# The words between the steps of a weight conversion, held in PSUM

## The chip, the core and the metric

The kernel runs on one core of a Trainium2 chip. Its engines are TensorE (PE: matmuls, PEld: weight loads), VectorE (DVE), ScalarE (ACT), GpSimd (POOL) and SyncE (SP, which issues all of the DMAs here). SBUF is the working memory; PSUM, eight banks of 128 partitions by 512 words of four bytes, takes what the matmuls write. The metric is the device time of one execution in microseconds.

## The reference

All of it is computed from float32 or float64 arrays of standard normal numbers, scaled. The weights arrive as 64-bit floats, seen by the kernel as pairs of 32-bit words.

```python
def sm_attn(qq, kk, vv):            # softmax attention, scale 1/sqrt(64)
    s = scale * np.matmul(qq, kk.transpose(0, 1, 3, 2))
    a = np.exp(s - np.max(s, axis=-1, keepdims=True))
    return np.matmul(a / (np.sum(a, axis=-1, keepdims=True) + 1e-09), vv)
p_packed = sm_attn(p, k, v)                  # 8 batches, 8 heads, 32 packed rows, 576 tokens
x = sm_attn(q, p_packed, p_packed)           # -> (4608, 512)
xn = x / np.sqrt(np.mean(x * x, axis=-1, keepdims=True) + 1e-06) * rms_g
g = xn @ w_gate                              # 512 -> 1536
x = (g * sigmoid(g) * (xn @ w_val)) @ w_out  # first MLP, 1536 -> 512
h = x @ w_in                                 # 512 -> 2048
out = (h * sigmoid(1.702 * h)) @ w_out2      # second MLP, 2048 -> 512
```

## The kernel before, in words

**Stages.** A start stage computes the attention of the first batches and begins the first MLP's weights. The first MLP (`mlp1`) then runs over four units `u` of two batches each, and within a unit over twelve slices `j` of 128 of the 1536 hidden columns. While it works on one unit, steps of the next unit's attention are put between its pieces; `run` yields the estimated nanoseconds of TensorE that a piece takes, and the main loop at the end spends them on attention steps. The second MLP (`mlp2`) comes last, over nine tiles of 512 tokens and sixteen slices of the 2048 hidden columns. The order of instructions on each engine is set by a scheduler at build time that starts from the order in the program and its own estimates of time; at run time every engine goes through its queue in order.

**Precision.** Most products are made of three matmuls on pairs "high, low" (`Wh, Wl` and so on): the high part is a rounded copy made by ScalarE, the low part is the difference, made by VectorE or GpSimd.

**PSUM.** Until the second MLP, pool `mm` has five banks under one tag, `mm`, handed out anew as they come free; pool `ap` has the other three for the attention. In the first MLP `mm` serves `ps_w` (L622, the slice's gate and value weights times the packed rows, read by ACT at L624 and DVE at L625), `ps_g` (L653, gate and value, read by ACT at L660 and DVE at L661 and L663) and `ps_o` (L684, the projection back to 512, read by ACT at L698 or L691, or DVE at L694). In the start stage, attention tiles take part of the `mm` banks too.

**Conversions.** `convert` makes a "high, low" pair out of raw 64-bit words: ScalarE takes the absolute value of the top words as a float (L105) into a tile `w`; VectorE works on it in four steps (L106 to L109: a lower bound, two shifts, the sign bits, the three bits from the low words); ScalarE makes the rounded copy (L110), and GpSimd the difference (L111). There are 104 conversions. In the first MLP `piece` converts its weights, 256 columns at a time, 72 in all, in the start stage and the first unit; the pairs go to DRAM and are read back for the later units. From the last unit on, `early` (in `mlp2`) converts the first nine slices of the second MLP's weights, 512 columns at a time, 18 in all, and `main` the other 14 when the second MLP runs and PSUM is laid out anew.

**POOL beside it.** GpSimd also makes `Hl` (L669) and adds into `acc` (L700) in the first MLP, in some 1.4 us each.

Of the kernel before, what the change touches and what calls it, by code (L numbers as in the profile page):

```python
# [9 lines left out]
F32 = mybir.dt.float32  # L10
F32R = mybir.dt.float32r
I32 = mybir.dt.int32
AF = mybir.ActivationFunctionType
ALU = mybir.AluOpType
# [5 lines left out]
LEAST_WORD = 2.0**-15  # L20


def fl(t):

    return t.bitcast(F32)
# [3 lines left out]
def tile_pack_attention__then__two_mlps(  # L29
# [14 lines left out]
    nc = tc.nc  # L44
    B, H, S, D = q.shape
    NP = p.shape[2]
    DM = H * D
# [6 lines left out]
    P = 128  # L54
# [40 lines left out]
    g_sb = const.tile([P, NPAIR], F32, name="g_sb")  # L95
    mhalf = const.tile([P, NC], F32, name="mhalf")

    def convert(pool, r, parts, n):


        top, low = r[:, :, 1], r[:, :, 0]
        w = pool.tile([P, n], I32, tag="w", name="w", bufs=3 if n < DM else 2)
        wf = w.bitcast(F32)
        shaped = wf if len(parts[0].shape) == 2 else wf.rearrange("p (i f) -> p i f", f=P)
        nc.scalar.activation(wf, top.bitcast(F32), AF.Abs)  # L105
        nc.vector.tensor_scalar(wf, wf, LEAST_WORD, None, op0=ALU.max)  # L106
        nc.vector.tensor_scalar(w, w, 5, 2, op0=ALU.logical_shift_left, op1=ALU.logical_shift_right)  # L107
        nc.vector.scalar_tensor_tensor(w, top, -(1 << 30), w, op0=ALU.bitwise_and, op1=ALU.bitwise_or)  # L108
        nc.vector.scalar_tensor_tensor(w, low, 29, w, op0=ALU.logical_shift_right, op1=ALU.bitwise_or)  # L109
        nc.scalar.copy(parts[0], shaped)  # L110
        nc.gpsimd.tensor_sub(parts[1], shaped, fl(parts[0]))  # L111

# [410 lines left out]
    def mlp1(cv, lp, mm, getL, getAT):  # L523
# [3 lines left out]
        HD = DM // 2  # L527
# [18 lines left out]
        raw = {}  # L546
# [20 lines left out]
        def piece():  # L567

            n = done[1]
            if n >= len(pieces):  # L570
                return False
            kind, j, c, h, _ = pieces[n]
            if j >= used[kind] + (WGB if kind == "wg" else G):
                return False
            done[1] += 1
            if (c, h) == (0, 0):
                tiles[kind, j] = new(kind, j)
            t = tiles[kind, j]
            if kind == "wg":
                parts = [t[:, x, 2 * h : 2 * h + 2, c * P : (c + 1) * P] for x in range(2)]  # L580
            else:
                parts = [t[:, x, h * HD : (h + 1) * HD] for x in range(2)]
            convert(cv, raw.pop(n), parts, HD)
            fetch()
            if n + 1 == len(pieces) or pieces[n + 1][:2] != (kind, j):
                nc.sync.dma_start((wg_d if kind == "wg" else wo_d)[j], fl(t))
                (wg if kind == "wg" else wo)[j] = tiles.pop((kind, j))
            return True

        def have(d, s):  # L590
            while s not in d:
                assert piece()
# [166 lines left out]
        return fetch, piece, run  # L759


    def mlp2(pre):
        xt = {}

        def load_x(t, pool):
# [18 lines left out]

        wi, wo = {}, {}
        raw = {}

        def load_w(n):
            f, x = divmod(n, 2)
# [17 lines left out]
                wi[f] = [w[:, y].rearrange("p (i f) -> p i f", f=P) for y in range(2)]  # L807

        def split_w(n, w):
            convert(pre, raw.pop(n), (w[:, 0], w[:, 1]), DM)  # L810
            load_w(n + 2)

        def keep(n, pool):
# [69 lines left out]
                    nc.sync.dma_start(out[t * TT + r * P : t * TT + (r + 1) * P, :], ob)  # L883

        def main(wp, xp):
            seq = [(t, f) for t in range(NTT) for f in range(NF2)]
            for n, (t, f) in enumerate(seq):
                if f == 2:
                    load_x(t + 1, pre if t % 2 else xp)
                if NF2 - 6 <= f < NF2 - 2:  # L890
                    split_x(t + 1, f + 6 - NF2)
                if t == 0:
                    if f == 0:
                        todo = list(range(4 + 2 * NEARLY, 2 * NF2))
                    for e in range(2, 5) if f == 0 else (f + 4,):
                        for x in range(2):
                            if e < 2 + NEARLY:
                                nc.sync.dma_start(fl(keep(2 * e + x, wp)), w2_d[e][:, x])
                up(t, f)
                if t == 0 and todo:  # L900
                    split_w(todo[0], keep(todo[0], wp))
                    todo.pop(0)
                if n >= 2:
                    down(*seq[n - 2])
            down(*seq[-2])
            down(*seq[-1])
# [5 lines left out]
    with ExitStack():  # L912
# [8 lines left out]
        with ExitStack() as st1:  # L921
            cv = st1.enter_context(tc.tile_pool(name="cv", bufs=1, side="left"))
            lp = st1.enter_context(tc.tile_pool(name="lp", bufs=1, side="left"))
            mm = st1.enter_context(tc.tile_pool(name="mm", bufs=MMB, space=PSUM, side="left"))
            st2 = ExitStack()
            ap = st2.enter_context(tc.tile_pool(name="ap", bufs=8 - MMB, space=PSUM, side="right"))
            at = st2.enter_context(tc.tile_pool(name="at", bufs=1, side="right"))
            Ls, ATs = {}, {}

            def begin(u):  # L930
                Ls[u] = tuple(lp.tile([P, NPAIR, P], F32R, tag=f"L{x}", name=f"L{x}", bufs=2) for x in "hl")
                ATs[u] = [
                    [lp.tile([P, S], F32, tag=f"AT{o}{g}", name=f"AT{o}{g}", bufs=1) for g in range(NG)]
                    for o in range(2)
                ]

            turn = [0]
            starting = [True]

            def psum():  # L940
                turn[0] += 1
                if starting[0] and turn[0] % 8 < MMB:
                    return mm.tile([P, 512], F32, tag="mm", name="ps_at")
                return ap.tile([P, 512], F32, tag="at", name="ps_at")

            def act(calls):
                for f, *args in calls:
                    f(*args)

            def unit(u):  # L950
                begin(u)
                n = 2 * NG * u
                seq = range(n, n + 2 * NG)
                return stages(seq, n + 2 * NG if u + 1 < NU else None, seq[NG - 1 :: NG])

            with tc.tile_pool(name="at2", bufs=1, side="left") as at2:
                start, stages = attention(at, [at2], lp, psum, Ls.get, ATs.get)
                fetch, piece, run = mlp1(cv, lp, mm, Ls.get, ATs.get)
                begin(0)
                todo = start(PERIOD, 2 * NG)  # L960
                while todo[0][0] < 0:
                    act(todo.pop(0)[1])
                nc.sync.dma_start(g_sb, rms_g.rearrange("(i p) -> p i", p=P))
                spent = CONV
                for _ in range(FETCH):
                    act(todo.pop(0)[1])
                for _ in range(3):
                    fetch()
                while todo[0][0] < LEADING:
                    time, calls = todo.pop(0)  # L970
                    act(calls)
                    while time > spent:
                        piece()
                        spent += PACE
                todo = [calls for _, calls in todo]
            starting[0] = False
            pools["main"] = st1.enter_context(tc.tile_pool(name="main", bufs=1, side="left"))
            u, ahead = 0, None
            every = EVERY / len(todo)
            spent, done = 0.0, 0.0  # L980
            for what in run():
                if what == "attention":
                    for calls in todo:
                        act(calls)
                    todo = []
                elif what == "next":
                    todo = unit(1)
                    every = 130000.0 / len(todo)
                elif what == "unit":
                    u += 1  # L990
                    if u + 1 < NU:
                        todo = unit(u + 1)
                        every = 143000.0 / len(todo)
                    elif u + 1 == NU:
                        st2.close()
                        pre = ctx.enter_context(tc.tile_pool(name="pre", bufs=1, side="right"))
                        early, second = mlp2(pre)
                        ahead = early()
                    spent = 0.0
                else:  # L1000
                    if ahead is not None and u == NU - 1:
                        next(ahead, None)
                    spent += what
                    done += what
                    while todo and spent >= every:
                        spent -= every
                        act(todo.pop(0))
                    while done >= PIECE:
                        done -= PIECE
                        piece()  # L1010
# [48 lines left out]
```

## Time and profile before

| | us |
|---|---|
| Time, median of three runs (1798.51 to 1803.16) | 1799.77 |
| The profiled execution's own time | 1803.39 |
| Its span, from the first to the last instruction | 1801.6 |
| PE busy | 1714.9 (95%) |
| DVE busy | 969.9 (54%) |
| ACT busy | 697.0 (39%) |
| POOL busy | 511.7 (28%) |

Durations come from one profiled execution on the chip. In the sliced view each digit is a slice's busy share in tenths (9 is 90% or more), and PEclk the granted clock of TensorE in tenths of full speed. In a group, the columns behind the shapes are the count, the engine's busy time in us, the mean ns of one instruction, and the engine's idle time just before them with what ended it. The ends of matmuls are modelled, so that neighbouring ones overlap in their records; neighbouring DVE instructions overlap by some 0.1 us too.

### The profile page before, as it was taken

The numbers are of one execution on the slowest core, as the hardware profiler recorded it, in microseconds if no ns is written. First come the engines' busy times: TensorE is split into PE (matmuls) and PEld (weight loads), VectorE is DVE, ScalarE is ACT, GpSimd is POOL, SyncE is SP. The second block draws the span as 40 slices with busy tenths as digits, with TensorE's granted clock in tenths as the row PEclk, the third lists the DMA queues.
The fourth block names the chain that finished last, engine by engine and source line by source line (L and its number), as shares of the span: only waits on it lengthen the run. The fifth ranks groups of instructions, "written<-read, shape, count | busy, mean of one in ns | idle before, by whom it ended". The sixth has DMA issues, their size and how long they took to land.

```text
span 1801.6 us, 26222 instructions
## 1 busy us (share of the span) xinstructions
PE 1714.9 (95%) x9976; PEld 1520.3 (84%) x9976; DVE 969.9 (54%) x1971; ACT 697.0 (39%) x1644; POOL 511.7 (28%) x470
## 2 busy tenths in 40 slices
PE   7798888999999999988899999999999999999998
PEld 5587877999999999978799788888888888888887
DVE  6979999856656666688955482122222222222221
ACT  5665655665555655556544331111111111111111
POOL 2546665644554345444544230000000000000000
PEclk9989998999999999999999999999999999999999
DMA  9654445454434542268731731010101010000000
GB/s 239 187 175 148 130 142 201 148 162 134 132 115 135 161 124 94 71 205 280 261 130 43 263 94 47 1 47 1 47 1 47 1 47 17 31 1 24 1 24 24
DMA packets 154462, 186.26 MB, mean 103 GB/s; under 512 B 87648, under 2 KB 124512, under 8 KB 147296
## 3 DMA queue, kind: packets, MB, share of 16 engines
q1 hardware_dynamic: 154336, 184.58, 32.0%
q8 instruction: 79, 1.29, 0.3%
q14 instruction: 47, 0.39, 0.1%
HBM read 139.46 MB, written 45.09 MB: 102 GB/s over the span
## 4 chain that ended last, share of the span: by engine, by line
PE 78%; DVE 16%; issue 2%; DMA 2%; ACT 2%; SPq 1%; POOL 0%; ACTq 0%; DVEq 0%; POOLq 0%
PE ps_dn L873 22%; PE ps_up L854 22%; PE ps_o L684 13%; PE ps_g L653 12%; DVE w L108 3%; PE ps_w L622 3%; DVE w L109 2%; PE ps_at L264 2%; DVE Wl L625 2%; DVE w L107 2%; DVE w L106 2%; PE ps_at L253 2%; DVE th L663 1%; PE ps_at L309 1%; DVE th L661 1%
## 5 line engine op out<-in xcount | busy, mean ns | idle before, releaser
L854 PE MATMUL ps_up<-xh,wi 128*128 128x512 f32 x1152 | 381.7, 393 | 2.3 <-DMA wi<-w 1.6
L873 PE MATMUL ps_dn<-wo,gh 128*128 128x512 f32 x1152 | 356.6, 391 | 0.0
L684 PE MATMUL ps_o<-Hh,wo 128*128 128x288 f32 x1536 | 332.1, 302 | 19.3 <-DVE th L661 9.0
L860 DVE CAST gh<-gf 128x512 fp32r<-128x512 f32 x144 | 62.4, 433 | 508.1 <-ACT gf L857 508.0
L857 ACT ACTIVATE gf<-ps_up 128x512 f32<-128x512 f32 x144 | 85.9, 597 | 610.3 <-PE ps_up L854 589.6
L684 PEld LDWEIGHTS ps_o<-Hh,wo 128*128 128x128 f32 x1536 | 255.5, 191 | 24.8 <-DVE th L661 9.9
L653 PE MATMUL ps_g<-Aqh,Wh 128*128 128x288 f32 x768 | 238.9, 312 | 23.5 <-ACT Wh L624 10.0
L854 PEld LDWEIGHTS ps_up<-xh,wi 128*128 128x128 f32 x1152 | 216.2, 188 | 52.0 <-POOL wo L111 2.0
L873 PEld LDWEIGHTS ps_dn<-wo,gh 128*128 128x128 f32 x1152 | 216.3, 188 | 47.5
L653 PE MATMUL ps_g<-Aql,Wh 128*128 128x288 f32 x768 | 229.5, 299 | 0.0
L684 PE MATMUL ps_o<-Hl,wo 128*128 128x288 f32 x768 | 228.2, 299 | 0.0
L653 PE MATMUL ps_g<-Aqh,Wl 128*128 128x288 f32 x768 | 228.1, 299 | 0.0
L854 PE MATMUL ps_up<-xl,wi 128*128 128x512 f32 x576 | 225.8, 392 | 0.0
L873 PE MATMUL ps_dn<-wo,gl 128*128 128x512 f32 x576 | 224.6, 391 | 0.0
L669 POOL TENSOR_TENSOR Hl<-th,Hh 128x576 fp32r<-128x576 f32 x96 | 141.0, 1469 | 235.4 <-ACT Hh L668 228.5
L653 PEld LDWEIGHTS ps_g<-Aqh,Wh 128*128 128x128 f32 x768 | 147.8, 193 | 32.0 <-ACT Wh L624 10.6
L700 POOL TENSOR_TENSOR acc<-acc,add 128x576 f32<-128x576 f32 x90 | 133.5, 1486 | 64.9 <-ACT add L698 64.8
L625 DVE TENSOR_TENSOR Wl<-ps_w,Wh 64x512 fp32r<-64x512 f32 x192 | 131.8, 687 | 30.9 <-ACT Wh L624 27.2
L653 PEld LDWEIGHTS ps_g<-Aql,Wh 128*128 128x128 f32 x768 | 147.8, 192 | 0.0
L653 PEld LDWEIGHTS ps_g<-Aqh,Wl 128*128 128x128 f32 x768 | 146.5, 192 | 0.5 <-DVE Wl L625 0.2
L684 PEld LDWEIGHTS ps_o<-Hl,wo 128*128 128x128 f32 x768 | 146.7, 191 | 0.1
L624 ACT CAST Wh<-ps_w 64x512 fp32r<-64x512 f32 x192 | 111.2, 580 | 59.5 <-PE ps_w L622 39.8
(146 smaller groups left out, 2649.2 us busy)
## 6 DMA issues: line engine op xcount, KB each, us to landing
wg<-wg SPq DMA_DIRECT2D x48, 1024.0 KB, 5.1
wo<-wo SPq DMA_DIRECT2D x48, 512.0 KB, 4.1
x<-acc SPq DMA_DIRECT2D x32, 288.0 KB, 2.4
out_dram<-ob SPq DMA_DIRECT2D x36, 256.0 KB, 2.0
vn<-in_v_dram SPq DMA_DIRECT2D x16, 512.0 KB, 5.3
qn<-in_q_dram SPq DMA_DIRECT2D x64, 128.0 KB, 4.0
raw<-in_moe_w_in_dram SPq DMA_DIRECT2D x16, 512.0 KB, 4.1
raw<-in_moe_w_out_dram SPq DMA_DIRECT2D x16, 512.0 KB, 3.8
```

Of the source, the lines that this page charges most:

```text
L108: nc.vector.scalar_tensor_tensor(w, top, -(1 << 30), w, op0=ALU.bitwise_and, op1=ALU.bitwise_or)
L622: nc.tensor.matmul(ps[:, a], st[:, i], mv[:, i], start=n == 0, stop=n == 2)
L624: nc.scalar.copy(Wh[rows, :, g], src)
L625: nc.vector.tensor_sub(Wl[rows, :, g], src, fl(Wh[rows, :, g]))
L653: nc.tensor.matmul(ps, st[:, o, g, c * P : (c + 1) * P], mv[:, g, cols], start=n == 0, stop=n == 3 * NG - 1)
L669: nc.gpsimd.tensor_sub(Hl, th, fl(Hh))
L684: nc.tensor.matmul(ps, st[:, m * P : (m + 1) * P], mv[:, cols], start=n == 0, stop=n == 3 * len(ss) - 1)
L700: nc.gpsimd.tensor_add(acc[o, m], acc[o, m], t)
L854: nc.tensor.matmul(ps, st[:, i], mv[:, i], start=n == 0, stop=n == 3 * NM - 1)
L857: nc.scalar.activation(gf, ps, AF.Gelu_apprx_sigmoid)
L860: nc.vector.tensor_copy(gh, gf)
L873: nc.tensor.matmul(pacc[r], st[:, r * P : (r + 1) * P], mv, start=f == 0 and n == 0, stop=f == NF2 - 1 and n == 2,)
```

## The change

`convert` gets a pool of banks. Where one is given, it takes a tile of 128 x 512 words of tag `mm` and uses its first `n` columns as `m`: L106 reads `w` in SBUF and writes `m` in PSUM, L107 and L108 read and write `m`, and L109 reads `m` and writes `w` in SBUF, from where L110 and L111 go on as before. The low and top words (`raw`) stay in SBUF. The number of instructions is the same. `piece` always gives `mm`; the second MLP's conversions give it while `early` runs and no longer once `main` does. In these the tile `m` is one more user of the five banks.

```diff
--- before.py
+++ after.py
@@ -95,18 +95,20 @@
     g_sb = const.tile([P, NPAIR], F32, name="g_sb")
     mhalf = const.tile([P, NC], F32, name="mhalf")
 
-    def convert(pool, r, parts, n):
+    def convert(pool, r, parts, n, banks=None):
+
 
 
         top, low = r[:, :, 1], r[:, :, 0]
         w = pool.tile([P, n], I32, tag="w", name="w", bufs=3 if n < DM else 2)
         wf = w.bitcast(F32)
         shaped = wf if len(parts[0].shape) == 2 else wf.rearrange("p (i f) -> p i f", f=P)
+        m = w if banks is None else banks.tile([P, 512], I32, tag="mm", name="between")[:, :n]
         nc.scalar.activation(wf, top.bitcast(F32), AF.Abs)
-        nc.vector.tensor_scalar(wf, wf, LEAST_WORD, None, op0=ALU.max)
-        nc.vector.tensor_scalar(w, w, 5, 2, op0=ALU.logical_shift_left, op1=ALU.logical_shift_right)
-        nc.vector.scalar_tensor_tensor(w, top, -(1 << 30), w, op0=ALU.bitwise_and, op1=ALU.bitwise_or)
-        nc.vector.scalar_tensor_tensor(w, low, 29, w, op0=ALU.logical_shift_right, op1=ALU.bitwise_or)
+        nc.vector.tensor_scalar(m.bitcast(F32), wf, LEAST_WORD, None, op0=ALU.max)
+        nc.vector.tensor_scalar(m, m, 5, 2, op0=ALU.logical_shift_left, op1=ALU.logical_shift_right)
+        nc.vector.scalar_tensor_tensor(m, top, -(1 << 30), m, op0=ALU.bitwise_and, op1=ALU.bitwise_or)
+        nc.vector.scalar_tensor_tensor(w, low, 29, m, op0=ALU.logical_shift_right, op1=ALU.bitwise_or)
         nc.scalar.copy(parts[0], shaped)
         nc.gpsimd.tensor_sub(parts[1], shaped, fl(parts[0]))
 
@@ -580,7 +582,7 @@
                 parts = [t[:, x, 2 * h : 2 * h + 2, c * P : (c + 1) * P] for x in range(2)]
             else:
                 parts = [t[:, x, h * HD : (h + 1) * HD] for x in range(2)]
-            convert(cv, raw.pop(n), parts, HD)
+            convert(cv, raw.pop(n), parts, HD, mm)
             fetch()
             if n + 1 == len(pieces) or pieces[n + 1][:2] != (kind, j):
                 nc.sync.dma_start((wg_d if kind == "wg" else wo_d)[j], fl(t))
@@ -759,7 +761,7 @@
         return fetch, piece, run
 
 
-    def mlp2(pre):
+    def mlp2(pre, banks):
         xt = {}
 
         def load_x(t, pool):
@@ -784,6 +786,7 @@
 
         wi, wo = {}, {}
         raw = {}
+        leading = [True]
 
         def load_w(n):
             f, x = divmod(n, 2)
@@ -807,7 +810,7 @@
                 wi[f] = [w[:, y].rearrange("p (i f) -> p i f", f=P) for y in range(2)]
 
         def split_w(n, w):
-            convert(pre, raw.pop(n), (w[:, 0], w[:, 1]), DM)
+            convert(pre, raw.pop(n), (w[:, 0], w[:, 1]), DM, banks if leading[0] else None)
             load_w(n + 2)
 
         def keep(n, pool):
@@ -883,6 +886,7 @@
                     nc.sync.dma_start(out[t * TT + r * P : t * TT + (r + 1) * P, :], ob)
 
         def main(wp, xp):
+            leading[0] = False
             seq = [(t, f) for t in range(NTT) for f in range(NF2)]
             for n, (t, f) in enumerate(seq):
                 if f == 2:
@@ -994,7 +998,7 @@
                     elif u + 1 == NU:
                         st2.close()
                         pre = ctx.enter_context(tc.tile_pool(name="pre", bufs=1, side="right"))
-                        early, second = mlp2(pre)
+                        early, second = mlp2(pre, mm)
                         ahead = early()
                     spent = 0.0
                 else:
```

## Rows read from the trace of the kernel before

**Rows 1.** The page's view in 40 equal slices.

```profile
PE   7798888999999999988899999999999999999998
...
DVE  6979999856656666688955482122222222222221
...
PEclk9989998999999999999999999999999999999999
```

**Rows 2.** Windows: busy us of PE, PEld, DVE, ACT, POOL; clock, DMA share, GB/s.

```profile
0.00:60.00 60.00, 48.26 (x232) 35.10 (x232) 40.21 (x120) 35.71 (x114) 20.30 (x40) 1.00 0.94 236
60.00:340.00 280.00, 235.49 (x1564) 218.13 (x1565) 258.24 (x548) 167.83 (x452) 165.62 (x166) 0.93 0.51 161
400.00:780.00 380.00, 380.00 (x2871) 370.87 (x2871) 244.00 (x552) 216.93 (x536) 177.20 (x159) 1.00 0.40 126
780.00:900.00 120.00, 98.36 (x672) 92.31 (x671) 110.79 (x179) 65.84 (x139) 57.64 (x38) 0.96 0.74 252
```

**Rows 3.** The chain of waits from 180 to 260 us: its shares by line.

```profile
by line: DVE w L108 13.7%; DVE w L109 10.3%; DVE Wl L625 9.0%; DVE w L107 8.6%; PE ps_g L653 7.9%; issue 7.1%; DVE th L661 5.0%; DVE th L663 4.5%; DVE w L106 4.3%; PE ps_w L622 3.7%; PE ps_at L264 3.5%; DVE kTl L134 2.6%; PE ps_at L412 2.3%
```

**Rows 4.** DVE's groups by shape, from 60 to 340 us.

```profile
L108 DVE SCALAR_TENSOR_TENSOR w<-raw,w 128x256 int32<-128x256 int32 x61 | 47.0, 774 | 0.3
L109 DVE SCALAR_TENSOR_TENSOR w<-raw,w 128x256 int32<-128x256 int32 x61 | 44.6, 734 | 0.4
L625 DVE TENSOR_TENSOR Wl<-ps_w,Wh 64x512 fp32r<-64x512 f32 x48 | 32.8, 686 | 1.5 <-ACT Wh L624 0.7
L107 DVE TENSOR_SCALAR w<-w 128x256 int32<-128x256 int32 x61 | 31.1, 511 | 0.4
L106 DVE TENSOR_SCALAR w<-w 128x256 f32<-128x256 f32 x61 | 27.4, 453 | 2.5 <-ACT w L105 2.4
...
L134 DVE TENSOR_TENSOR aTl<-ps_at,aTh 128x256 fp32r<-128x256 f32 x8 | 3.4, 420 | 0.5 <-ACT aTh L132 0.5
```

**Rows 5.** DVE's groups by shape, 780 to 900 us.

```profile
L108 DVE SCALAR_TENSOR_TENSOR w<-raw,w 128x512 int32<-128x512 int32 x20 | 18.4, 918 | 0.4
L109 DVE SCALAR_TENSOR_TENSOR w<-raw,w 128x512 int32<-128x512 int32 x19 | 18.3, 963 | 0.1
...
L107 DVE TENSOR_SCALAR w<-w 128x512 int32<-128x512 int32 x20 | 17.0, 852 | 0.2
L106 DVE TENSOR_SCALAR w<-w 128x512 f32<-128x512 f32 x20 | 13.3, 664 | 7.6 <-ACT w L105 7.4
```

**Rows 6.** Two lines, whole span: shortest, median and longest ns.

```profile
L661 DVE SCALAR_TENSOR_TENSOR th<-th,ps_g x192: 383/452/456, 81.0 to 986.5; 128x288 f32<-128x288 f32 x192
...
L108 DVE SCALAR_TENSOR_TENSOR w<-raw,w x104: 404/684/2502, 17.4 to 1070.3; 128x256 int32<-128x256 int32 x72, 128x512 int32<-128x512 int32 x32
```

**Rows 7.** Timeline of DVE, 200 to 230 us: start us, duration us.

```profile
202.35 0.28 DVE L107 TENSOR_SCALAR w<-w 128x256 int32<-128x256 int32 x1
...
205.98 0.28 DVE L106 TENSOR_SCALAR w<-w 128x256 f32<-128x256 f32 x1
...
206.88 0.42 DVE L109 SCALAR_TENSOR_TENSOR w<-raw,w 128x256 int32<-128x256 int32 x1
...
216.48 1.52 DVE L109 SCALAR_TENSOR_TENSOR w<-raw,w 128x256 int32<-128x256 int32 x1
```

**Rows 8.** Timeline of POOL, 200 to 230 us.

```profile
216.12 1.59 POOL L700 TENSOR_TENSOR acc<-acc,add 128x576 f32<-128x576 f32 x1
```

**Rows 9.** Windows of three parts at clock 0.83: first, and sum.

```profile
60.00:100.00 40.00, 25.31 (x131) 21.38 (x131) 36.92 (x83) 24.10 (x66) 20.99 (x25) 0.83 0.52 162
...
sum 100.00, PE 77.56 PEld 70.28 DVE 93.65 ACT 54.91 POOL 60.01; mean PE 25.85 PEld 23.43 DVE 31.22 ACT 18.30 POOL 20.00
```

**Rows 10.** Timeline of DVE, 805 to 835 us.

```profile
813.02 0.73 DVE L106 TENSOR_SCALAR w<-w 128x512 f32<-128x512 f32 x1
...
817.14 0.68 DVE L109 SCALAR_TENSOR_TENSOR w<-raw,w 128x512 int32<-128x512 int32 x1
```

**Rows 11.** The chain of waits from 180 to 260 us, in order of time.

```profile
184.60 0.79 PE ps_g L653 x6
```

## The prediction

> **What bounds the kernel now.** I read the sliced view first: PE's digits are 9 almost from end to end, with two dents, one near the start and one near the middle, and DVE's row shows its 8s and 9s in just those places [rows 1]. The windows turn this into microseconds [rows 2]. From 400 to 780 us PE is busy for all 380 us and DVE for 64% of the time: PE is the bound there. From 60 to 340 us PE is busy for 235.5 of 280 us while DVE is busy for 258.2, and from 780 to 900 us PE for 98.4 of 120 while DVE has 110.8. Those two stretches hold 44.5 + 21.6 = 66.1 us of PE's idle time, and that is what a relief of DVE can win at most, apart from the clock. The chain of waits says whether DVE really sets the pace: from 180 to 260 us the four conversion lines (L106 to L109) carry 13.7 + 10.3 + 8.6 + 4.3 = 36.9% of it, far ahead of any matmul line [rows 3].
>
> The groups of DVE's instructions then give what to price [rows 4, 5]. In the first stretch 61 conversions of 256 columns cost 453 + 511 + 774 + 734 = 2472 ns each, 150 us of DVE's 258. In the second, 18 of the leading kind (512 columns) cost 664 + 852 + 918 + 963 = 3397 ns each (the group shows 20 and 19, since up to two later ones, which the change leaves alone, begin inside the window).
>
> **Why these are dear.** The means are not the instructions' own size. On a free moment the same lines at 256 columns take 0.28 us (L106), 0.28 (L107) and 0.42 (L109) [rows 7]; L108 goes from 404 ns to 2502 ns over both sizes [rows 6]. The long cases coincide with POOL: L109 at 216.48 us took 1.52 us [rows 7], and POOL ran L700 from 216.12 for 1.59 us [rows 8], so L109 ended 0.3 us after POOL, about what it needs by itself. By contrast L661, which has one operand in PSUM and one in SBUF, never left 383 to 456 ns in 192 instances [rows 6], though POOL was as busy beside it. So I read the excess as DVE being held off while POOL works, for SBUF-only instructions and not for those with a PSUM input. At free prices a conversion is 2 x 0.28 + 2 x 0.42 = 1.40 us, so 1.07 us of the 2.47 is excess.
>
> [...]
>
> **The change part by part.** It adds no instruction and no DMA, and moves nothing in a queue by itself. It swaps an operand's place: L106 writes PSUM, L107 reads and writes it, L108 reads raw from SBUF and the word from PSUM and writes PSUM, L109 reads both and writes SBUF.
>
> Price after. No DVE instruction of the trace writes PSUM. The nearest rows read it: 420 ns for L134 at 256 columns, 686 ns for L625 at 512 [rows 4], 452 ns (median) for L661 at 288 [rows 6]. I take 0.42 us for all four, 1.68 us a conversion. The low end is that the writes cost nothing and the first two keep 0.28 us: 1.40 us. The high end is today's L107 mean with its waits, 0.51 us four times: 2.04 us. At 512 columns I take 4 x 0.686 = 2.74 us; low, with the first two at the same ratio 0.28/0.42 to it, 2.29; high, nothing saved, 3.40.
>
> So DVE sheds 61 x (2.47 - 1.68) = 48 us in the first stretch (26 to 65) and 18 x (3.40 - 2.74) = 12 us in the second (0 to 20). DVE's totals become 210 and 99 us. Now PE is the next to bind: 235.5 and 98.4 us. The 11 conversions before 60 us gain nothing I count: DVE has 40.2 of 60 us there and the DMA share is 0.94 [rows 2].
>
> [...] No run here shows the write side.
>
> How much of PE's idle time goes. PE cannot go to 100%: the attention's chains remain, and the start is thin. If PE reaches 95% in the first stretch, it lasts 235.5 / 0.95 = 248 us, 32 us less. [...] At full clock those 77.6 us would be 64, 13 us less; I count 6. In the second stretch both engines stand near 99 us; at 90% it lasts 110, a gain of 10. Sum 48 us.
>
> Against it stands the ring. A conversion now takes one of five banks from L106 to the end of L109. The one at 813.02 us would hold its bank until 817.82, 4.8 us [rows 10], and conversions overlap: one's L106 at 205.98 stands ahead of another's L109 at 206.88 [rows 7]. 61 x 4.8 / 280 is about one bank held on the average, two at times, so the matmuls keep three to four. A gate tile takes PE 0.79 us to fill [rows 11] and some 0.45 us on DVE to read, or an activation more; filling, waiting and reading in turn need two to three banks if the readers are prompt. Mostly enough, not always. I charge 8 us for PE waiting at a full ring. Net 40 us.
>
> This is against the profiled execution: 1803.4 us, of which the span is 1801.6. Its time lies 3.6 us above the median of the runs, 1799.8, so the forecast for the median is 1799.8 - 40 = 1760 us. Within 0.3% (5.4 us) I call it no change: the three runs spread by 0.26%.
>
> The wait that is added: L106 must have its bank free. Behind it on DVE stand L625, L661 and L663, for which ACT, POOL and PE wait. POOL and SP are not moved past anything; POOL, no longer blocked by these four lines, can only gain.
>
> **The rivals.**
>
> *The ring is too small.* Relief arrives on DVE, but PE waits for banks in its place. For it: when DVE lags, all of the ring is wanted. Against: from 400 to 780 us PE is never short of a bank, and faster conversions free the others' banks sooner. If this eats three quarters of the 48 us, 12 us remain: 1788.
>
> *DVE waits in line for its bank (slower).* L106 stands in order; if its bank's last tile is still being filled (0.79 us) and read by ACT (some 0.4 us, if an activation is like L661's instance on DVE), the whole DVE queue stands for up to 1.2 us. It decides against the change once the mean wait passes the relief, 0.79 us in the first stretch. At the full 1.2 us, (1.2 - 0.79) x 61 + (1.2 - 0.66) x 18 = 35 us on an engine that already fills the stretch: 1835. At 0.9 us it is 11, or 1811. Against it: most of the earlier tiles' readers stand before L106 on DVE itself, so it need not wait for them.
>
> *PSUM costs its rate and does not lift the hold.* That the excess is not POOL's doing, or that a write to PSUM is held off too. Then the four cost 1.68 + 1.07 = 2.75 us instead of 2.47: 61 x 0.28 = 17 us and as much again per element in the second stretch, 18 x 0.4 = 7: 1824. The rows of L661 speak against it; that none writes PSUM leaves it open. If only half of the excess stays, 1.68 + 0.54 = 2.22 us, 15 us of relief, some 1788.
>
> **How the numbers follow.** My forecast, with its own range from 1731 (all at the good end: PE at 97% in both stretches, so 37 + 19 us, with the whole 13 us of clock and no loss at the ring, 69 us) to 1785 (the high price of 2.04 us in place of 1.68, which leaves about half of DVE's relief, and the loss at the ring in full), has 0.70. The ring too small, or half the excess staying, 1785 to 1805: 0.15, of which half falls within 0.3% of no change. DVE waiting in line: 0.10. The hold not lifted: 0.05. Faster 0.70 + 0.08 = 0.78, same 0.07, slower 0.15. The range for 8 in 10 is 1738 to 1798: the two slower cases lie above it, with a small part of the others on either side.
>
> **What would show it.** Right: L106 to L109 near 0.42 us (256 columns) and 0.69 us (512) with hardly a long case; PE above 93% in the stretch that ends with the last first-MLP conversion, which ends some 35 to 40 us earlier; DVE's busy sum down by about 60 us; and a second dent 10 us shorter. The clock's share would show as fewer slices below 9. Wrong: idle time of DVE ahead of L106 put down to ACT or PE (the queue stands), PE waiting more at the ring for readers while DVE is idle (the ring), or L106 to L109 still with cases over 1 us beside POOL (the hold remains).

## The result, and the profile after

The changed kernel takes 1771.76 us in the median of four runs (1770.43 to 1774.51), against 1801.47 for the kernel before (four runs beside it): a ratio of 0.9839, 95% interval 0.9817 to 0.986. That is 29.7 us, or 1.6%, less. The forecast was 1760, within 1738 to 1798, so the time lies in the range and 11.8 us above the forecast. The profiled execution has a span of 1772.7 us, 28.9 less than before. The lines of `convert` stand two lower in the new file: L107 is the absolute value on ACT, L108 to L111 are DVE's four steps, L112 and L113 the two parts.

The page, first three rows of the sliced view and then the chain of waits of the whole span, by engine and by line:

```profile
PE   7899989999999999999998999999999999999998
...
DVE  5688898746756566667875662222222222222221
...
PEclk9899999999999999999999999999999999999999
```

```profile
PE 80%; DVE 9%; DMA 5%; ACT 3%; issue 2%; SPq 1%; POOL 0%; DVEq 0%; ACTq 0%; POOLq 0%
PE ps_dn L876 22%; PE ps_up L857 22%; PE ps_o L686 14%; PE ps_g L655 11%; PE ps_at L266 2%; PE ps_w L624 2%; DVE Wl L627 2%; PE ps_at L311 2%; PE ps_at L388 2%; PE ps_at L255 1%; DMA raw<-in_moe_w_in_dram 1%; DVE th L663 1%; DMA raw<-in_moe_w_gate_dram 1%; DVE between L110 1%; DMA raw<-in_moe_w_val_dram 1%
```

Against [rows 1] PE's first dent has two 8s left behind the opening 7, where it had a 7 and four 8s, and the middle one is a single 8 in place of three; DVE's 8s and 9s there have thinned out. In the chain DVE has 9% and DMA 5%, where the kernel before has

```profile
PE 78%; DVE 16%; issue 2%; DMA 2%; ACT 2%; SPq 1%; POOL 0%; ACTq 0%; DVEq 0%; POOLq 0%
```

No conversion step stands among the first lines but one at 1%, and three kinds of raw words do. The windows say how much time all this is. The columns are as in [rows 2]; the third stretch is wider than there, because the second MLP's conversions now reach beyond 930 us:

```profile
0.00:60.00 60.00, 45.96 (x198) 32.10 (x199) 35.21 (x111) 31.06 (x98) 16.61 (x34) 0.94 0.88 222
60.00:340.00 280.00, 255.71 (x1727) 232.27 (x1726) 235.30 (x605) 186.07 (x508) 167.99 (x184) 0.96 0.56 171
...
740.00:960.00 220.00, 207.10 (x1518) 201.13 (x1518) 163.57 (x311) 122.40 (x255) 100.56 (x75) 0.99 0.54 188
```

From 60 to 340 us PE is busy for 255.7 us, 20.2 more than in [rows 2], and DVE for 235.3 in place of 258.2. Up to 60 us PE is busy for 46.0 in place of 48.3: the start has become a little worse. Over the whole span PE's idle time goes from 1801.6 - 1714.9 = 86.7 us to 1772.7 - 1713.1 = 59.6, so 27 of the 29 us are idle time that is gone, and PE's own busy time has hardly moved (1.8 us).

DVE's steps by themselves, from 60 to 340 us at 256 columns and then from 780 to 940 us at 512 (columns as in [rows 4, 5]):

```profile
L110 DVE SCALAR_TENSOR_TENSOR between<-raw,between 128x256 int32<-128x256 int32 x62 | 25.9, 420 | 0.5
L109 DVE TENSOR_SCALAR between<-between 128x256 int32<-128x256 int32 x61 | 25.8, 424 | 0.6
L111 DVE SCALAR_TENSOR_TENSOR w<-raw,between 128x256 int32<-128x256 int32 x62 | 25.3, 410 | 0.8
L108 DVE TENSOR_SCALAR between<-w 128x256 f32<-128x256 f32 x60 | 25.1, 419 | 8.6 <-ACT w L107 3.5 <-ACT add L700 3.5 <-ACT acc L693 1.3
```

```profile
L108 DVE TENSOR_SCALAR between<-w 128x512 f32<-128x512 f32 x18 | 12.5, 693 | 9.5 <-ACT acc L693 6.1 <-ACT add L700 3.0
L109 DVE TENSOR_SCALAR between<-between 128x512 int32<-128x512 int32 x18 | 12.5, 693 | 0.2
L110 DVE SCALAR_TENSOR_TENSOR between<-raw,between 128x512 int32<-128x512 int32 x18 | 12.4, 689 | 0.1
L111 DVE SCALAR_TENSOR_TENSOR w<-raw,between 128x512 int32<-128x512 int32 x18 | 12.2, 679 | 0.3
```

A conversion of 256 columns is 419 + 424 + 420 + 410 = 1673 ns where it was 2472, and one of 512 is 2754 ns where it was 3397. The long cases are gone; the third step, which ran from 404 to 2502 ns [rows 6], now shows

```profile
L110 DVE SCALAR_TENSOR_TENSOR between<-raw,between x90: 391/423/695, 17.2 to 931.0; 128x256 int32<-128x256 int32 x72, 128x512 int32<-128x512 int32 x18
```

with 695 ns, the price of 512 columns, as its longest of 90. DVE's busy time falls from 969.9 to 912.2 us. In the same place where [rows 3] showed four conversion steps, from 180 to 260 us, the chain now reads

```profile
by line: DMA raw<-in_moe_w_val_dram 14.6%; PE ps_g L655 12.0%; DMA raw<-in_moe_w_gate_dram 11.5%; PE ps_o L686 6.2%; issue 5.7%; PE ps_at L311 4.9%; DMA raw<-in_moe_w_out_dram 4.6%; DVE Wl L627 3.9%; ACT w L107 3.7%; PE ps_w L624 2.7%; DVE 
```

and its largest part by far, 14.6 + 11.5 + 4.6 = 30.7%, is the transfer of raw words. Nothing in the prediction speaks of that. The last conversion of the first MLP ends at 338.0 us, as good as where it did before, at 338.6 (the ends of L111 and L109 there).

### The profile page after: what moved, and what is told of

Its sections match the earlier page's. It is cut to its first block, busy times and chain, and to the rows that moved or that the text cites. A ratio compares the mean times of both kernels' runs of the same rounds, so it can differ in the third digit from the quotient of the medians.

```text
span 1772.7 us, 26286 instructions
## 1 busy us (share of the span) xinstructions
PE 1713.1 (97%) x9976; PEld 1513.4 (85%) x9976; DVE 912.2 (51%) x1971; ACT 699.5 (39%) x1644; POOL 495.8 (28%) x470
## 4 chain that ended last, share of the span: by engine, by line
PE 80%; DVE 9%; DMA 5%; ACT 3%; issue 2%; SPq 1%; POOL 0%; DVEq 0%; ACTq 0%; POOLq 0%
PE ps_dn L876 22%; PE ps_up L857 22%; PE ps_o L686 14%; PE ps_g L655 11%; PE ps_at L266 2%; PE ps_w L624 2%; DVE Wl L627 2%; PE ps_at L311 2%; PE ps_at L388 2%; PE ps_at L255 1%; DMA raw<-in_moe_w_in_dram 1%; DVE th L663 1%; DMA raw<-in_moe_w_gate_dram 1%; DVE between L110 1%; DMA raw<-in_moe_w_val_dram 1%
## 5 line engine op out<-in xcount | busy, mean ns | idle before, releaser
L702 POOL TENSOR_TENSOR acc<-acc,add 128x576 f32<-128x576 f32 x90 | 129.9, 1444 | 69.1 <-ACT add L700 68.5
```

What stands on the lines that cost most here:

```text
L702: nc.gpsimd.tensor_add(acc[o, m], acc[o, m], t)
```

## The experiments

Each run stands beside runs of the kernel before on the same chip; the ratios are to those, with 95% intervals. In one table, in the order of the text:

| run | median us | ratio to before | interval |
|---|---|---|---|
| the change | 1771.8 | 0.9839 | 0.9817 to 0.986 |
| first MLP's conversions alone | 1779.6 | 0.9873 | 0.9845 to 0.9901 |
| second MLP's conversions alone | 1792.7 | 0.9937 | 0.9916 to 0.9959 |
| POOL's long work taken away, SBUF | 1759.6 (one run) | | |
| first two steps in PSUM | 1770.6 | 0.9825 | 0.981 to 0.9841 |
| third word alone in PSUM | 1795.8 | 0.9968 | 0.9953 to 0.9982 |
| before, ring of four | 1816.1 | 1.0081 | 1.0064 to 1.0098 |
| changed, ring of four | 1787.0 | 0.9907 | 0.9881 to 0.9933 |
| changed, but SBUF in the start stage | 1756.8 | 0.9732 | 0.9703 to 0.9762 |
| the same, two banks held in the start | 1753.4 | 0.9717 | 0.97 to 0.9733 |
| changed, four buffers of raw words | 1753.3 | 0.9721 | 0.97 to 0.9742 |
| SBUF in the start, four buffers | 1753.8 | 0.9724 | 0.9708 to 0.9741 |
| before, four buffers | 1808.5 | 1.0037 | 1.0022 to 1.0052 |

My theory was that the gain is DVE no longer held off by POOL, stretch by stretch. The rivals were, for the gain, that it came from a new order of the instructions, which the scheduler makes anew for each program, and, for the part that was missing against the forecast, that the ring gave it back.

### Each half of the change alone

```diff
-            convert(pre, raw.pop(n), (w[:, 0], w[:, 1]), DM, banks if leading[0] else None)
+            convert(pre, raw.pop(n), (w[:, 0], w[:, 1]), DM)
```

> Only the first MLP's 72 conversions use PSUM; the second MLP's 18 early ones stay in SBUF. Theory (DVE is no longer held off, and each dent pays for itself): the first dent's share alone, some 17 us of PE's idle time, so 1785 us, and the second dent as before (PE busy near 82% of its 120 us, L107 to L111 near 3.4 us a conversion there). Rival (the gain is the new order that the scheduler makes, one for the whole program): anything between 1772 and 1801, with no relation to the stretch that was changed.

```diff
-            convert(cv, raw.pop(n), parts, HD, mm)
+            convert(cv, raw.pop(n), parts, HD)
```

> Only the second MLP's 18 early conversions use PSUM; the first MLP's 72 stay in SBUF. Theory: the second dent's share alone, 10 to 13 us, so 1789 us, with the first dent as before (PE idle 44 us from 60 to 340 us). The gains of this run and of the first MLP's alone then add up to the 29 us of the change. Rival (order): they don't add up.

By the ratios they save 1.27% and 0.63% (22.9 and 11.4 us of 1801), 34 in sum where both together save 1.61% (29 us): they add up within the intervals, which are some 5 us wide to either side. The undone stretch stays as it was. Windows of the kernel before, then of the first alone, then of the second alone, from 740 to 960 us (and from 60 to 340 in the last):

```profile
740.00:960.00 220.00, 196.79 (x1418) 189.77 (x1418) 173.05 (x305) 116.97 (x252) 101.45 (x73) 0.98 0.55 188
```

```profile
740.00:960.00 220.00, 198.08 (x1429) 190.75 (x1428) 173.01 (x299) 115.86 (x247) 100.30 (x69) 0.98 0.53 188
```

```profile
60.00:340.00 280.00, 237.28 (x1542) 220.34 (x1542) 256.55 (x545) 167.68 (x453) 164.19 (x167) 0.91 0.51 159
740.00:960.00 220.00, 211.07 (x1551) 204.94 (x1551) 161.78 (x313) 124.33 (x266) 102.44 (x78) 0.99 0.51 179
```

PE's 196.8 us there become 198.1 where the second MLP's conversions stay in SBUF and 211.1 where only they are moved; and that run's first stretch still has 237.3 us of PE beside 256.6 of DVE. So the gain sits where the conversions are, as the theory has it. The order of instructions agrees with that: on PE, DVE, ACT and POOL the second alone has the very order of the kernel before up to 764 us at least, and the first alone that of the changed kernel, so a new order elsewhere in the program didn't bring these gains. Within a changed stretch the order is new too, and no run tells it from the steps' price there. The first half saved more than the 17 us that I expected of it.

### What lifts the hold

First POOL's long work of the conversions and of the first MLP is taken out of the kernel before, which leaves out a part of the computation; this run is read for DVE's steps, not for its time.

```diff
-        nc.gpsimd.tensor_sub(parts[1], shaped, fl(parts[0]))
+        nc.scalar.copy(parts[1], shaped)
...
-            nc.gpsimd.tensor_sub(Hl, th, fl(Hh))
+            nc.scalar.copy(Hl, th)
...
-                        nc.gpsimd.tensor_add(acc[o, m], acc[o, m], t)
+                        nc.scalar.copy(acc[o, m], t)
```

> The kernel before, with POOL's three long instructions of the first MLP and the conversions (the weights' low part, the hidden rows' low part, the adding into acc) replaced by plain copies on ACT; so part of the computation is left out, the low parts and the sums are not made. Theory (POOL holds DVE off): the four SBUF steps fall to their free prices at 256 columns, 0.28, 0.28, 0.42 and 0.42 us on the mean, with few long cases (the attention's POOL work remains). Rival (the long cases have another cause, as the raw words' stride or DMA): they stay at 0.45, 0.51, 0.77 and 0.73 us. The time itself says little, since ACT has some 250 us more to do.

DVE's groups of that run from 740 to 900 us, where POOL is busy for 1.2 us in all, and then the 256-column ones from 60 to 340 us, where the attention's work is left on POOL (52.5 us in place of 165.6):

```profile
L108 DVE SCALAR_TENSOR_TENSOR w<-raw,w 128x512 int32<-128x512 int32 x20 | 13.7, 687 | 0.3
L109 DVE SCALAR_TENSOR_TENSOR w<-raw,w 128x512 int32<-128x512 int32 x20 | 13.7, 684 | 0.1
...
L106 DVE TENSOR_SCALAR w<-w 128x512 f32<-128x512 f32 x20 | 8.5, 425 | 13.4 <-ACT w L105 13.3
L107 DVE TENSOR_SCALAR w<-w 128x512 int32<-128x512 int32 x20 | 8.4, 421 | 0.3
```

```profile
L108 DVE SCALAR_TENSOR_TENSOR w<-raw,w 128x256 int32<-128x256 int32 x61 | 29.5, 487 | 0.5
L109 DVE SCALAR_TENSOR_TENSOR w<-raw,w 128x256 int32<-128x256 int32 x61 | 29.1, 479 | 0.4
...
L106 DVE TENSOR_SCALAR w<-w 128x256 f32<-128x256 f32 x61 | 21.1, 348 | 12.2 <-ACT w L105 12.1
L107 DVE TENSOR_SCALAR w<-w 128x256 int32<-128x256 int32 x61 | 20.3, 336 | 0.3
```

All four steps in SBUF, and without POOL they cost 425, 421, 687 and 684 ns at 512 columns where [rows 5] has 664, 852, 918 and 963. At 256 columns, where the expectation named 0.28 and 0.42 us, they come down from 453, 511, 774 and 734 ns [rows 4] only to 348, 336, 487 and 479, with part of POOL's work still there. So the excess goes with POOL's work; the words' stride is the same as before, and the DMA share no lower (0.57 from 60 to 340 us, against 0.51 [rows 2]).

Then only the first two steps' words lie in PSUM, or only the third's:

```diff
-        nc.vector.scalar_tensor_tensor(m, top, -(1 << 30), m, op0=..., op1=...)
-        nc.vector.scalar_tensor_tensor(w, low, 29, m, op0=..., op1=...)
+        nc.vector.scalar_tensor_tensor(w, top, -(1 << 30), m, op0=..., op1=...)
+        nc.vector.scalar_tensor_tensor(w, low, 29, w, op0=..., op1=...)
```

> Only the first two steps' words lie in PSUM; the third step reads PSUM and writes SBUF, and the fourth has two SBUF inputs again, so the bank is held for a shorter time. [...] Rival (it is the write into SBUF that POOL holds off): the third step is long as well.

```diff
-        nc.vector.tensor_scalar(m.bitcast(F32), wf, LEAST_WORD, None, op0=...)
-        nc.vector.tensor_scalar(m, m, 5, 2, op0=..., op1=...)
-        nc.vector.scalar_tensor_tensor(m, top, -(1 << 30), m, op0=..., op1=...)
+        nc.vector.tensor_scalar(wf, wf, LEAST_WORD, None, op0=...)
+        nc.vector.tensor_scalar(w, w, 5, 2, op0=..., op1=...)
+        nc.vector.scalar_tensor_tensor(m, top, -(1 << 30), w, op0=..., op1=...)
```

> [...] Theory (the inputs decide): step three keeps its long cases and its 0.77 us although it writes PSUM, and so do steps one and two; step four alone comes to 0.42 us. Relief 0.3 us of 0.79: some 1790 us. Rival (the output decides): step three is at 0.42 us with no long case, and step four is long.

The third and fourth steps (L110, L111) from 60 to 340 us, first of the former, then of the latter, there with the first two (L108, L109) as well:

```profile
L111 DVE SCALAR_TENSOR_TENSOR w<-raw,w 128x256 int32<-128x256 int32 x61 | 42.6, 700 | 0.5
...
L110 DVE SCALAR_TENSOR_TENSOR w<-raw,between 128x256 int32<-128x256 int32 x61 | 25.1, 411 | 1.0
```

```profile
L110 DVE SCALAR_TENSOR_TENSOR between<-raw,w 128x256 int32<-128x256 int32 x60 | 44.0, 734 | 3.4 <-ACT add L700 2.4 <-ACT acc L693 0.2
L108 DVE TENSOR_SCALAR w<-w 128x256 f32<-128x256 f32 x60 | 38.3, 638 | 10.5 <-ACT w L107 10.2
L109 DVE TENSOR_SCALAR w<-w 128x256 int32<-128x256 int32 x60 | 35.1, 586 | 0.7
...
L111 DVE SCALAR_TENSOR_TENSOR w<-raw,between 128x256 int32<-128x256 int32 x59 | 24.2, 410 | 0.5
```

A step with one input in PSUM and one in SBUF costs 410 or 411 ns, and writing to SBUF does it no harm. A step with both inputs in SBUF costs 700 or 734 ns, and writing to PSUM doesn't save it. So in these two runs the inputs decide, and not the output as both rivals had it. The times did not follow the sums so well. In the former a conversion is 418 + 422 + 411 + 700 = 1951 ns, which is 0.52 us of relief where the whole change has 0.80, and by that share of its 29.7 us I would estimate 1782 us; it came to 1770.6, no slower than the whole change. The latter came to 1795.8 where 1790 was expected. There the first two steps, left in SBUF, cost 638 and 586 ns where they had cost 453 and 511 [rows 4], so that a conversion is 2368 ns and only 0.10 us are won where 0.3 were expected, which goes with the time; why they became dearer is not shown. The former frees its bank after the third step; that this makes up for its dear fourth step was not tested by itself.

### What a bank costs

```diff
-            mm = ...tile_pool(name="mm", bufs=MMB, space=PSUM, side="left"))
+            mm = ...tile_pool(name="mm", bufs=MMB - 1, space=PSUM, side="left"))
```

> The kernel before with a ring of four banks, the fifth left unused and the conversions in SBUF: the price of one bank, without the relief. If a bank is dear, 1810 us or more; if the matmuls can spare it, 1801 to 1805 us.

> The changed kernel with a ring of four banks, the fifth left unused. If the ring is what ate the missing 11 us of my forecast (a conversion holds one bank on the average and the matmuls are short of the rest), one bank less costs more than that one did: 1785 us or more. If the ring is wide enough, 1772 to 1777 us.

One bank less costs the kernel before 0.8% (15 us) and the changed one 0.7% (12 us by the ratios, 15 by the medians): a bank is dear to either. Part of the price falls where no conversion runs at all, from 360 to 740 us, first before and then changed; PE was busy for all of it with five banks:

```profile
360.00:740.00 380.00, 372.88 (x2781) 359.52 (x2779) 237.41 (x545) 214.17 (x540) 177.35 (x164) 1.00 0.41 132
```

```profile
360.00:740.00 380.00, 376.98 (x2826) 365.88 (x2825) 232.74 (x530) 211.08 (x521) 170.89 (x154) 1.00 0.40 130
```

In sum the changed kernel doesn't suffer more than the other. Its 1787.0 us reach the 1785 that were to speak for the ring, but as the kernel before pays as much, that mark decides nothing. Where the price falls does differ: in the conversions' stretches, from 60 to 340 and from 740 to 960 us, PE's busy time changes by -2.1 and +1.3 us in the kernel before, by -5.3 and -1.9 in the changed one. With one trace of each, it stays open how much the conversions tighten the ring. On DVE's side the wait that the change adds, L108 for a bank that ACT has yet to read, is small on the whole. Waits of DVE in the changed kernel, with their sum, number and longest in us:

```profile
DVE between L108 <- ACT acc L693: 7.5, 4, 4.8
...
DVE between L108 <- ACT add L700: 6.5, 5, 1.6
```

That is 14.0 us in 9 cases, 0.16 us for each of 90 conversions, where it took 0.79 to turn the change around. In the second stretch by itself, from 780 to 940 us, it is 9.1 us for 18 conversions, 0.5 us each, not far from the 0.66 that was the price there. But DVE had stood there for ACT before as well: its idle time ahead of the first step goes from 7.6 us [rows 5] to 9.5.

### The start stage

In the changed kernel the first gate matmul comes late. One line's matmuls, before and after: the figures behind the durations are the starts of the first and the last in us.

```profile
L653 PE MATMUL ps_g<-Aqh,Wh x768: 288/295/609, 72.1 to 986.2; 128*128 128x288 f32 x192
```

```profile
L655 PE MATMUL ps_g<-Aqh,Wh x768: 288/294/579, 90.8 to 957.3; 128*128 128x288 f32 x192
```

72.1 us became 90.8, while the last one came early. So the next kernel keeps the conversions of the start stage in SBUF:

```diff
-            convert(cv, raw.pop(n), parts, HD, mm)
+            convert(cv, raw.pop(n), parts, HD, None if main is None else mm)
```

> The first MLP's conversions use PSUM only once the start stage is over; there, where attention tiles take banks of the same ring, they stay in SBUF. Theory as it stands (the start stage gave part of the gain back, the first gate matmul coming at 91 us in place of 72, because its attention tiles had fewer banks): the first gate comes at about 72 us again, and the time falls by up to 10 us below the changed kernel, to 1762 us. Rival (the start stage loses nothing by the ring; the gates were only put later in the order): 1772 us or more, up to 1778, as the start's 20 or so conversions are held off by POOL again at 0.8 us each.

It takes 1756.8 us, 15 less than the change, where 10 were expected at most, and the first gate is back:

```profile
L655 PE MATMUL ps_g<-Aqh,Wh x768: 288/295/609, 73.8 to 941.7; 128*128 128x288 f32 x192
```

I had put that down to attention tiles that lack banks. The next run tests this: the kernel just shown, with two banks of the ring taken and held through the start.

```diff
+                held = [mm.tile([P, 512], F32, tag="mm", name="held") for _ in range(2)]
+                for h in held:
+                    nc.vector.memset(h[:, :1], 0.0)
...
+                for h in held:
+                    nc.vector.tensor_add(mhalf_x, h[:, :1], fl(Ls[0][0])[:, NPAIR - 1, :1])
```

> The same kernel (start stage in SBUF), but two banks of the ring are taken at the outset and held until the first packed rows are done, just ahead of the first ps_w: the shortage of banks in the start by itself, without a conversion in PSUM (two tiny VectorE instructions more at either end). If the changed kernel loses its 15 us in the start because attention tiles lack banks (on the chip, or in the scheduler's order, which goes by the same ring), this run loses as much: 1768 us or more, the first gate matmul at 85 us or later. If the loss is in the order by another cause, 1757 to 1761 us and the first gate near 74 us.

It loses nothing, 1753.4 us, with the first gate at 74.0:

```profile
L656 PE MATMUL ps_g<-Aqh,Wh x768: 288/295/610, 74.0 to 944.9; 128*128 128x288 f32 x192
```

So, at least with its conversions in SBUF, the start can spare two banks, and that explanation falls. The other trace of the loss was on ACT. Waits of ACT for the raw words of the first MLP's gate and value weights, in the kernel before and in the changed one (sum, number, longest):

```profile
ACT w L105 <- DMA raw<-in_moe_w_val_dram: 6.3, 7, 2.4
...
ACT w L105 <- DMA raw<-in_moe_w_gate_dram: 4.6, 5, 2.2
```

```profile
ACT w L107 <- DMA raw<-in_moe_w_val_dram: 17.8, 12, 3.5
...
ACT w L107 <- DMA raw<-in_moe_w_gate_dram: 13.7, 14, 3.7
```

10.9 us became 31.5. In the start such a wait can hold up the attention, as the changed kernel's timeline shows from 65 to 72 us (lines of ACT, then one of PE):

```profile
68.11 0.43 ACT L107 ACTIVATE w<-raw 128x256 f32<-128x256 f32 x1 [2.73 <-DMA raw<-in_moe_w_gate_dram]
...
71.00 0.39 ACT L134 COPY kept<-ps_at 128x256 f32<-128x256 f32 x1
...
71.44 4.21 PE L266 MATMUL ps_at<-qTh,kept 128*128 128x256 f32 x8 [3.36 <-ACT kept L134]
```

ACT stood 2.73 us for raw words, then worked without a gap through what had queued up, down to the copy of `kept` at 71.00, and PE stood 3.36 us for that copy. A fourth buffer of raw words lets a fetch begin earlier:

```diff
-            r = cv.tile([P, HD, 2], I32, tag="raw", name="raw", bufs=3)
+            r = cv.tile([P, HD, 2], I32, tag="raw", name="raw", bufs=4)
...
-                for _ in range(3):
+                for _ in range(4):
                     fetch()
```

> The changed kernel with four buffers of raw words for the first MLP in place of three. In its start stage ACT stands 15 us before L107 for raw words (4.5 us before the change), with the attention's copies queued behind. If those waits are what the start loses, most of the 15 us comes back: about 1760 us, the first gate near 75 us. If not, 1768 to 1774 us.

> The kernel of the run that keeps the start stage's conversions in SBUF, with four buffers of raw words for the first MLP in place of three. After the change ACT stands 17 us before L107 for raw words between 120 and 360 us (5 to 8 us before the change). If that new wait holds part of the gain, it shrinks and the time falls by some 5 us below 1757; if it is idle time of an engine off the path, 1755 to 1759 us.

> The kernel before with four buffers of raw words for the first MLP in place of three: the control for the run that gave the changed kernel a fourth buffer and 18 us. If the fourth buffer pays because the change made the conversions wait for raw words, it brings nothing here, where VectorE is the bound and ACT stood only 12 us before L105 for raw words up to 360 us: 1797 to 1805 us. If the fourth buffer helps the start stage whatever the change, 1785 us or less.

The changed kernel falls by 18 us to 1753.3, below the 1760 expected. Its first gate comes at 79.8 us, earlier than 90.8 but not near 75:

```profile
L655 PE MATMUL ps_g<-Aqh,Wh x768: 288/294/445, 79.8 to 934.9; 128*128 128x288 f32 x192
```

The waits for gate and value words are down to one of 0.3 us, and the raw words are gone from the chain of 180 to 260 us, which is now led by matmuls:

```profile
ACT w L107 <- DMA raw<-in_moe_w_val_dram: 0.3, 1, 0.3
```

```profile
by line: PE ps_o L686 24.7%; PE ps_g L655 22.8%; PE ps_at L311 5.4%; PE ps_at L388 4.8%; issue 4.2%; PE ps_at L255 3.9%; PE ps_w L624 3.8%; DVE between L109 2.6%; DVE between L108 2.5%; DVE between L110 2.2%; DVE kTl L136 2.2%; PE ps_at L26
```

The start's windows from 40 to 60 and 60 to 80 us, of the changed kernel and then of this one, show a difference in the granted clock too (the column behind the busy times):

```profile
40.00:60.00 20.00, 18.19 (x73) 12.88 (x74) 13.15 (x40) 11.83 (x44) 7.38 (x13) 0.83 0.78 225
60.00:80.00 20.00, 15.06 (x51) 9.95 (x50) 12.08 (x29) 7.27 (x27) 8.90 (x16) 0.75 0.72 187
```

```profile
40.00:60.00 20.00, 18.56 (x87) 13.56 (x88) 15.86 (x47) 13.83 (x49) 9.33 (x18) 1.00 0.82 237
60.00:80.00 20.00, 15.25 (x67) 10.46 (x67) 16.28 (x35) 13.56 (x43) 8.31 (x13) 0.91 0.51 136
```

0.83 and 0.75 became 1.00 and 0.91. They are means: taken by half microseconds from 35 to 90 us, the changed kernel's clock is 1.00 in 68 windows, 0.50 in 37 and something between in 5. In the 40 us from 40 to 80 PE is busy for much the same time, 33.3 and 33.8 us, but gets through 124 and 154 matmuls; in the 40 us ahead of that it was busy for 27.8 and 28.9 us. Of the 21.5 us between the two spans, 1772.7 and 1751.2, half, 10.8 us, is PE's own busy time (1713.1 to 1702.3) for the same matmuls, while the mean granted clock of the execution goes from 0.990 to 0.994. That the clock makes this difference is my estimate: no run changes the clock by itself.

The kernel with SBUF in the start gains at most 3 us by the fourth buffer (1756.8 to 1753.8; the intervals overlap), so the two cures don't add up, as if both removed the same loss. The kernel before gains nothing by the buffer; it becomes 0.37% slower, 1808.5 us where 1805 was expected at most. The loss, then, belongs to the change: conversions in PSUM and three buffers of raw words together.

The traces don't place the two gains alike, though. The first gate matmul of the second unit starts at 357.4 us in the changed kernel, at 340.3 with SBUF in the start and at 335.0 with four buffers. SBUF in the start is 17 us ahead at the first gate of all and 17 here; the fourth buffer is 11 us ahead at the first and 22 here, so half of its gain lies behind the start, in the stretch where raw words led the chain. This is a coarse measure: the first MLP alone, with the changed kernel's order up to 764 us, has the two gates at 86.5 and 350.4 us, 4 and 7 us ahead of it.

What stays open is which way the loss comes about: by ACT's standing on the chip, or by the order that the scheduler made (the changed kernel's queue has the first conversions ahead of copies that the attention needs). Every cure changed the order as well, and no run held it fixed: up to 72.8 us the kernel with SBUF in the start has the very order of the kernel before on PE, DVE, ACT and POOL. Nor did any run give the second MLP's raw words more buffers than their two; ACT stands 18.3 us for its `w_in` words in the changed kernel and 12.2 in the one before.

## Why the prediction was right

**What bounds the kernel, and why the steps were dear:** right. With POOL's long work gone the steps come down in SBUF as well, at 256 columns from 2472 to 1650 ns a conversion, and with one input in PSUM the long cases end: 695 ns is the third step's longest where 2502 was. The kind of the inputs decides, 410 or 411 ns against 700 or 734. POOL, which could "only gain", did: its busy time goes from 511.7 to 495.8 us.

**The price after:** right. Forecast 1.68 and 2.74 us, measured 1.673 and 2.754. No write to PSUM had been seen; it costs what a read does, 419 to 424 ns at 256 columns where L134, which reads it, took 420 [rows 4]. Beside a busy POOL a conversion of 256 columns cost 2.47 us in SBUF and 1.67 in PSUM. Without POOL's long work SBUF was the cheaper place: at 512 columns 425 + 421 + 687 + 684 = 2217 ns against 2754.

**DVE's relief:** right, 57.7 us of busy time in the whole span, where 48 + 12 = 60 was the sum.

**How much of PE's idle time goes:** right in the second dent, too high in the first. The second gave 11 us alone, where 10 were counted. The first gave 23 us alone, where 32 + 6 were, less the ring's share. The step that failed is "If PE reaches 95% in the first stretch": it reached 255.7 of 280 us, 91%, so that 20.2 us of idle time went and not 32. No run shows the clock's 6 us, counted out of 13 by the ratio 0.83 [rows 9]; what the runs show in their place is PE's busy time, which fell by 1.8 us (with four buffers of raw words by 12.6), and a mean granted clock of 0.985 before, 0.990 after and 0.994 with four buffers. Two of the signs named for being right failed with it: PE above 93%, and the last conversion of the first MLP 35 to 40 us earlier, which came 0.6 us earlier. "Now PE is the next to bind" left out what feeds the conversions. Behind DVE stood the raw words, with three buffers: ACT's wait for them nearly trebled (10.9 to 31.5 us for gate and value). Two different runs give back 15 and 18 us; how much of that is ACT's standing, and how much the order, stays open. With the loss cured the saving is 2.8%, 50 us, which is more than the 40 net of the forecast and close to the 48 before the ring's charge.

**The ring:** no run isolates the 8 us charged for it. The hold itself was reckoned well, although the 4.8 us came from a conversion of 512 columns in the second stretch: from L108's start to L111's end a bank is held for 4.1 us on the mean at 256 columns, which makes 0.94 banks from 60 to 340 us. A bank is worth some 15 us to this kernel, but to the one before just as much; DVE's queue stood 14.0 us for a bank in all; and with four buffers of raw words all conversions are in the ring as well, yet the saving is 50 us. So the ring isn't what kept the change from its forecast.

**The rivals:** DVE in line for its bank was there at a fifth of its deciding price over all conversions (0.16 of 0.79 us), and at three quarters of it in the second stretch. The hold not lifted was excluded by the steps' rows after the change. The sign and the range held. That the time came within 12 us of the forecast is in part luck: the first stretch and, by PE's busy time, the clock fell short by 12 and 4 us, and the 8 us for the ring made up for half of that.

## What to carry to other kernels

Where VectorE and GpSimd work at once, look at the spread of one line's durations, not at its mean alone: the line that ran from 404 to 2502 ns here was being held off, and an operand moved to PSUM paid although the first two steps cost 0.42 us there and 0.28 on a free moment in SBUF [rows 7]. When a change speeds up a step, ask at once what feeds it: here three buffers did for the slow step, and a fourth was worth 18 us after the change and cost 7 before it.

## What the runs showed of the hardware

With the words between them in PSUM, VectorE's four steps cost the same whether PSUM is written, read or both: 419, 424, 420 and 410 ns at 256 columns, 679 to 693 at 512. For the first two that gives up a faster rate: in SBUF they took 0.28 us at 256 columns on a free moment [rows 7], and 425 and 421 ns at 512 without POOL's long work. An output in PSUM doesn't free an instruction with two SBUF inputs beside a busy POOL: 734 ns on the mean, as against 774 with all three in SBUF [rows 4], and up to 2337 ns.
